# Rebuilding float32 weights from float64 words on Trainium2: the clamp of the high word left out, its scale changed, and a new order of work

## The chip, the cores and the metric

The kernel runs on one core of one Trainium2 chip. The metric is the device time of one execution in microseconds (us), the median of three runs: 724.92 us before the change (723.97 to 729.51). TensorE does the matrix products and transposes, VectorE (DVE in the profile) and ScalarE (ACT) the elementwise work, GpSimd (POOL) elementwise work that they can spare, and the queues of SyncE (SP) and ScalarE start the DMA transfers.

## The reference

A clustered attention feeds two dense blocks in a row. Queries and keys are assigned to the nearest of 16 centroids, and a query sees only the keys of its own cluster:

```python
q_assign = np.argmax(np.einsum('bhsd,hcd->bhsc', q_n, c_n), axis=-1)
k_assign = np.argmax(np.einsum('bhsd,hcd->bhsc', k_n, c_n), axis=-1)
mask = q_assign[:, :, :, None] == k_assign[:, :, None, :]
scores = np.where(mask, scale * np.matmul(q, k.transpose(0, 1, 3, 2)), -1000000000.0)
attn = softmax(scores)             # q, k, v: (2, 8, 768, 64)
x = attn @ v                       # as (1536, 512)
h = x @ w_in                       # (512, 2048)
g = np.where(h >= 1, h, np.where(h <= -1, 0.0, (h + 1) ** 2 / 4))
x = g @ w_out                      # (2048, 512)
h = ((x @ w1) * (x @ w2)) @ w3     # (512, 1024) twice, (1024, 1024)
return h @ w_out2                  # (1024, 512)
```

The activations are float32. The five weight matrices arrive as float64.

## The kernel before, in words

**Stages.** The work is cut by the two elements of the batch. Batch 0's attention comes first (four units of two heads; a unit has 12 score blocks of 128 queries by 768 keys). Beside it the kernel multiplies w3 by w_out2 once (the 16 products of line 1207). Then batch 0's dense work (line 1277: `h`, `y`, `ab` and `o` products) runs on TensorE with batch 1's attention mixed in, and last batch 1's dense work, in part as seven products for eight (line 1530). A score block goes TensorE (line 860), row maximum on VectorE (line 868), a bias on GpSimd (line 873), exponential on ScalarE (line 881), transposes on TensorE (line 898), a copy out of PSUM (line 353 on ScalarE, 355 on VectorE), and its PSUM buffer is then free for another. In batch 0 there are four such score buffers.

**A weight chunk.** A chunk is a 128x512 block of float64, that is 128x1024 words of 32 bits in a ring `w64` of five buffers early and three later. There are 72 such chunks: 8 of w_out2, 16 of w3 and 48 of the rest, which are rebuilt once, kept in DRAM (`wd`) and read back as float32 for batch 1. `chunk` (line 1098) makes these steps of each:

1. `wl` (line 1106): a DMA, started from ScalarE's queue, brings the 512 KB.
2. `wabs` (line 1112): ScalarE takes the absolute value of the high words, read as float32, times 2^16, into a buffer of the ring `wf`. The upper 8 of the 11 exponent bits of a float64 stand where a float32 has its exponent, so that this scale adds 16 to them.
3. `clamp` (line 1116, step `("wc", i, 0)`): VectorE (68 chunks) or GpSimd (4 chunks) holds the result between two powers of two, in place.
4. `wr` (line 1122): ScalarE scales and rounds the low words.
5. `shift_low` (line 1126): VectorE shifts the high word left by 3 bits and ORs the low word's bits in.
6. `sign` (line 1132): VectorE ORs the sign bit in. The 32 bits are then the weight as float32, and the `w64` buffer is free.
7. For a chunk that is multiplied at once: `whi` (lines 353 and 355) rounds it to TensorE's reduced float32 into a buffer of the ring `whl` (three buffers), on ScalarE or VectorE, and `wlo` (line 358) subtracts that from the weight, on GpSimd or VectorE.

**What sets the order.** Every step is handed to a small planner with the engines that may do it. `Plan.order` (line 127) then takes no decision of its own: it reads the string `ORDER` (lines 38 to 97), two letters a step, that says which step is next and on which of its engines. Engines run their instructions in that order, each on its own, and wait for each other by semaphores.

Of the kernel before, what the change touches and what calls it, by code (L numbers as in the profile page):

```python
# [38 lines left out]
    "###%#*#,#0#($V%X%[:m$X$.#.#2#6$0#4$6%e%h$8$:%V%b$<$_%c%q$a$>$c$e$4$2#g;#;4#_%]%_%i%y&,%|%k&#:s;D:o%m#L$H$@#m"  # L39
    "#8$J$g$B$L$Z$]$q$s$F;%;)$N;T&($D;*#B;:#o#X$*$i#q$o$P$u$k:q$m#|#@#P#e#w#k$R$%%s%u$T%w;J:u$w;6;F%o#y#c)u#a#J#<"  # L40
    "#N#F#D$()w)y$y$|)|:w:y:|*4;g;Z;,;.;y*(***,#>*##T*%*6*8;1;2$##]#i#R#V;8&**.*@*B*D*:%#;m*F#:*<;<*0;H;>;A;B*2*>"
    ";L#s*L*H*N*P*X#Z*Z*];V;X;i;N;k&&;o;Q;q*J$,#H#u*u;s*R*T+4&>*_*e;|<#*g;R*a*V*c+(+**w+6;];_*m<%<(<*<2&.+,*y&0&:"
    "*|+@+.+#+&+8+:+<<D<4<6;a;c<V+0+2+>+L&3*i*k<i+B+D+N+P+X+Z+]*o<8<:&7&5<<<>+F+R&G*q+_<F<H<-+e<.*s<y;e;v&K+H+T+u"
    "+a+J+V+c,(+w,4,6,*<J&8&<&I<]<X<k+m+y+|,#,L,8,:,,,.=2=%<Z<_<L<m&M<N<Q<R;w%>%(<a<c,0,%,2,@,B,D,X&N,N&D<o<q=D,<"
    ",>,Z<s<0<A<|=V,F<B=#=(,u,P,R+g+i+l=*,T,H+o=8,],_,a<u<w=i=4,J,V,w,y,|+r=J=6,e=:=<=,=.=>&Q<T<f<g-#-%,c&@-(-*+s"
    "-4-6=y=o>2=F=H-,-.&C-8,g=L=X=Z&c-:&j=0=@=B=N=]=_=a=c-0-2=P=R=k-@,i-<-L-B-D-X-Z-]>%&T>D-N-P=|>#=m&_-F->>(=q=s"
    ">V&k>4,k=u=w>8>i>*>,>.>6-R&X,m,o-H-u-K-w,r-y>:&S><>>=T=e=g>|-T,s%%.(.*%@-_>J>F-V>H>X>Z>L>]-|>_&W>a>c>N>0-a&e"
    "-c?4>@>k&o>B.#-e&^.4.6>m&a&[%*>Q.%>o>q>S>s&n?D.,..?(-m&s-g-i-k?:>u>w.8.0.@.B.D.3-o>T>f>g.L.N?T?#?%?*?6?8&g?,"
    "?.?<?F?H-q.:&u?g.F.X.<.P.R.T?J?Z?>?|?V.H.Z.J?L.W?X@4.>?N.]._>y?@?0.u?2.a?m.c%B?]?Q/4/(?_?a?C?S/@/6-s.w/B/*@H"
    "&y(&?u?c?e?w?y&q@Z(#@(?i&w(-%,@#?k@%&|?o(((.%D/8.y.|@6@8@*.e/:?q?s/,/./D@,@:@<.m@J@L@>@@/#/%@N@P@R/</0/2@o/>"  # L50
    "%.%0%2%4@.@0/F@T@V/L%F%H.g/N/P%6%J/H@BA(A<@a@]@`/J@u@i@2AN@D%L(*%8/R@q@F/X/Z(4.i.k/]%:.o@c@s%<%N@e@g/_/e@w/g"
    "/T/V@X@k.q.s@m/a/cABA*@y@|AcAuA./u0(/w/y0*/|0,0.A>A,A0A#APA604%P06%RA@A2A4%T/mARADAFATAVAXAZ08000#0%020:A%A8"
    "A:0<0@AHAK0>0L0N0PAe/i/k0XAiAg0B0DB0AkAmAp0u0wAqA|0R0FA]B*ALA_Aa0Z0]AwAyBBB#0T0HBV0J/o/rB20_0y0|B6AsB,B4B.(0"
    "1#0a0V1(0c(2/s0eB8B%B:(61*1,0gB(BDBF1416BHBi18BJBL0m1.10BXBZB]B_Ba1%BNBPB<B>121X1ZBw1]0i0kBd1:1@1L(:Be1N1P1B"
    "1DBk(8(=(>B@BRBT1RBo(A1<1T(B(L1FC#0o0r0s1_1>(NBm1e1gBqBg1H1J1VByB|1a1d(D(FCBBsBu(H(J1i1lC%2*2,2.201u1w1y1|(P"
    "(RCaD%23241m1o1r(T1s(V2#2%2628(XCDCG2(C(C*C,C.(ZCd2:2<C0C6C8C:C32>DD2F2HD)2JC52@2B2DD*C<C?C@GDCTCV2L2O2P2RCX"
    "CeCHCJCZDFCL2T2VDcCN2XD,D.D0D2CQE(2c2eE6C]2Z2]2gCR2i2_D4C_2lCsCuCwCyDH2a2mCgCiDeDh2oD8D:D6D<D>C|CkE*CmG_3%3("
    "3*DJDLDOD#3436E,3,3/3032DiDVE9EDGJER3P3R2y(]CoEaDPDkDADCCrE.383:3<3>3@DmDXD[D]Do3T3VE:F%D_3Y3Z3]3B3D3F(b(d(_"
# [35 lines left out]
    "hBgYjDiRhqiUh4hDg_gagZhuhwh,hyi_iai%h0h>h8isi(hHhLi4hFi[i^h:j)hsi,icieiwhki*jFjNhNiui6hPh~j,ihiii|hJhRilipjH"
    "imjahThVi8i:i.i>jPjdi<j.iBiDjeiFiqj*iyj#jLj0i0i@iHjRj%j6jJjgjij4j2j>j8j;j<jTjAjkjmjojBiJiLjZjqk#j^k.k&k@k)k*"
    "jwk,k0kBk3kEkHkFkJjyj|j_jWjXkLk:k<k>jtjukNk4kPkRk6k8kTkVkXkZ"
# [44 lines left out]
def cluster_attention_moe_kernel(  # L141
# [961 lines left out]

# [692 lines left out]
```

## Time and profile before

| | |
|---|---|
| median of the runs | 724.92 us (723.97 to 729.51) |
| profiled execution | 726.57 us, its span 724.9 us |
| busy share of the span | TensorE 97%, VectorE 87%, ScalarE 67%, GpSimd 39% |
| granted TensorE clock, mean | 0.998 of full speed |

The span runs from the first to the last instruction of the program; 1.7 us of the profiled execution lie around it. A TensorE that is shown busy is not one at its peak, since its instructions overlap and their ends are modelled. The shares are means over stages that differ: ScalarE is shown busy for 156.7 us of the 175 us from 25 to 200 us, and for 4.1 us of the last 25 us.

### The profile page before, as it was taken

The page shows a single profiled execution, that of the slowest core. Times are in us where ns is not written, and L with a number is a line of the kernel's source. Part 1 is how long each engine was busy: PE and PEld are TensorE (multiplying, and loading weights), DVE is VectorE, ACT ScalarE, POOL GpSimd, SP SyncE. Part 2 cuts the span into 40 slices and gives each one's busy share as a digit, 9 for nine tenths or more (in the row PEclk, how much of TensorE's full clock was granted, in tenths as well). Part 3 has the DMA queues.
Part 4 walks back from the last instruction along what each step waited for, and adds up shares of the span by engine and source line. Part 5 has one row for each costly group of instructions (what it writes and reads, how often), then busy time and mean ns, then how long its engine had stood idle before and what let it go on. Part 6 is the DMA issues. An engine that isn't in the chain of part 4 may idle for free.

```text
span 724.9 us, 12096 instructions
## 1 busy us (share of the span) xinstructions
PE 700.6 (97%) x4184; PEld 632.5 (87%) x4185; DVE 631.0 (87%) x1135; ACT 482.9 (67%) x897; POOL 283.4 (39%) x351
## 2 busy tenths in 40 slices
PE   4999999899999999999999999999999999999998
PEld 1867777577799999899989999999999999999997
DVE  6999999999988989999999999578988888999940
ACT  7989999988877897887877766335744444444201
POOL 3424334313544523522351532134644433267600
PEclk9999999999999999999999999999999999999999
DMA  8346687877789999897898788554212121222112
GB/s 315 97 158 218 215 260 234 278 236 235 198 200 204 198 218 222 205 246 196 217 225 248 212 207 216 140 171 147 74 58 74 59 87 45 60 70 62 58 44 102
DMA packets 122509, 121.58 MB, mean 168 GB/s; under 512 B 80656, under 2 KB 89296, under 8 KB 122448
## 3 DMA queue, kind: packets, MB, share of 16 engines
q1 hardware_dynamic: 99888, 61.39, 33.6%
q10 hardware_dynamic: 22560, 59.42, 26.4%
q8 instruction: 33, 0.54, 0.3%
q14 instruction: 28, 0.23, 0.1%
HBM read 75.79 MB, written 22.28 MB: 135 GB/s over the span
## 4 chain that ended last, share of the span: by engine, by line
PE 74%; DVE 6%; ACT 3%; issue 2%; DMA 0%; POOL 0%; DVEq 0%; SPq 0%; ACTq 0%; POOLq 0%
PE mo L1277 36%; PE sc L1277 7%; PE sc L1530 6%; PE sc L860 6%; PE mo L1530 5%; PE mo L1207 3%; PE av L977 3%; PE sc L898 2%; PE av L1277 2%; PE av L969 2%; PE av L1530 2%; ACT pt L353 1%; DVE wf L1132 1%; DVE tv L1441 1%; ACT P L881 1%
## 5 line engine op out<-in xcount | busy, mean ns | idle before, releaser
L1277 PE MATMUL mo<-X,whl 128*128 128x384 f32 x912 | 168.2, 339 | 0.6 <-DVE tmp L1302 0.4
L1277 PEld LDWEIGHTS mo<-X,whl 128*128 128x128 f32 x912 | 158.6, 188 | 3.7 <-DVE tmp L1302 0.7
L358 POOL TENSOR_TENSOR whl<-wf,whl 128x512 fp32r<-128x512 f32 x64 | 86.1, 1346 | 113.5 <-ACT whl L353 79.6
L1277 PE MATMUL mo<-G,whl 128*128 128x384 f32 x660 | 122.5, 340 | 0.2 <-DVE G L358 0.2
L1277 PEld LDWEIGHTS mo<-G,whl 128*128 128x128 f32 x660 | 116.0, 188 | 1.9 <-issue 0.6
L868 DVE TENSOR_REDUCE nm<-sc 128x1 f32<-128x768 f32 x96 | 89.6, 951 | 7.5 <-PE sc L860 6.5
L353 ACT ACTIVATE whl<-wf 128x512 fp32r<-128x512 f32 x84 | 52.5, 628 | 46.6 <-PE mo L1277 19.6
L873 POOL TENSOR_SCALAR nm<-nm 128x1 f32<-128x1 f32 x96 | 29.7, 310 | 132.2 <-DVE nm L868 128.2
L860 PE MATMUL sc<-k,q 128*128 128x512 f32 (+1 forms) x192 | 53.4, 359 | 5.4 <-ACT pt L353 2.7
L1122 ACT ACTIVATE w<-w,down 128x512 uint32<-128x512 uint32 x72 | 54.8, 768 | 0.4 <-ACT whl L353 0.3
L1112 ACT ACTIVATE wf<-w 128x512 f32<-128x512 f32 x72 | 47.9, 672 | 6.8 <-POOL whl L358 2.6
L1132 DVE SCALAR_TENSOR_TENSOR wf<-w,wf 128x512 uint32<-128x512 uint32 x72 | 51.6, 721 | 0.8
L1126 DVE SCALAR_TENSOR_TENSOR wf<-wf,w 128x512 uint32<-128x512 uint32 x72 | 50.0, 698 | 2.2 <-ACT w L1122 1.0
L881 ACT ACTIVATE P<-sc,nm 128x768 f32<-128x768 f32 x52 | 46.5, 900 | 7.3 <-POOL nm L873 1.9
L881 ACT ACTIVATE sc<-sc,nm 128x768 f32<-128x768 f32 x44 | 38.1, 867 | 19.4 <-POOL nm L873 19.2
L860 PE MATMUL sc<-kq 80*128 80x512 f32 (+1 forms) x192 | 49.5, 339 | 0.0
L358 DVE TENSOR_TENSOR phl<-sc,phl 128x768 f16<-128x768 f32 x44 | 41.9, 953 | 4.9 <-ACT phl L353 4.6
L898 PEld LDWEIGHTS sc<-ident,P 128*128 128x128 f32 x312 | 36.0, 143 | 11.1 <-ACT P L881 7.3
L898 PE MATMUL sc<-ident,P 128*128 128x128 f32 x312 | 42.6, 281 | 3.0 <-ACT P L881 2.7
L358 POOL TENSOR_TENSOR wh<-ws,wh 128x256 fp32r<-128x256 f32 x42 | 34.0, 817 | 25.5 <-ACT wh L353 14.8
L1277 PE MATMUL sc<-G,whl 128*128 128x384 f32 x240 | 43.7, 339 | 0.0
L1277 PEld LDWEIGHTS sc<-G,whl 128*128 128x128 f32 x240 | 42.5, 188 | 0.0
(241 smaller groups left out, 1478.0 us busy)
## 6 DMA issues: line engine op xcount, KB each, us to landing
wf<-wd ACTq DMA_DIRECT2D x64, 256.0 KB, 2.8
w<-in_w_out_dram ACTq DMA_DIRECT2D x24, 512.0 KB, 4.3
wd<-wf SPq DMA_DIRECT2D x48, 256.0 KB, 3.3
w<-in_w3T_dram ACTq DMA_DIRECT2D x16, 512.0 KB, 4.3
w<-in_w_in_dram ACTq DMA_DIRECT2D x16, 512.0 KB, 4.9
w<-in_w_dram ACTq DMA_DIRECT2D x16, 512.0 KB, 4.1
wp<-wf SPq DMA_DIRECT2D x16, 256.0 KB, 3.0
wf<-wp ACTq DMA_DIRECT2D x16, 256.0 KB, 2.9
```

The source lines that it names most:

```text
L353: nc.scalar.activation(out=out, in_=in_, func=AF.Copy)
L358: (nc.gpsimd if e == "POOL" else nc.vector).tensor_tensor(out=out, in0=a, in1=b, op=ALU.subtract)
L860: nc.tensor.matmul(ps[:, n], q[0:n_rows, q0:q0 + 128], k[0:n_rows, n], start=first, stop=not first)
L868: nc.vector.tensor_reduce(out=nm, in_=T[("sc", b), s], axis=AX.X, op=ALU.max, negate=True)
L881: nc.scalar.activation(out=new(("P", b), s).rearrange("p n s -> p (n s)") if by_pe(s) else T[("sc", b), s], in_=T[("sc", b), s], func=AF.E ...
L898: nc.tensor.transpose(T[("sc", b), s][:, c], p[:, c], ident)
L1112: nc.scalar.activation(out=T["wf", i], in_=T[w64, i].bitcast(F32)[:, :, 1], func=AF.Abs, scale=1.0 if by_add else float(2.0 ** 16))
L1122: nc.scalar.activation(out=lo, in_=lo, func=AF.Identity, scale=float(2.0 ** -29 - 2.0 ** -41), bias=down)
L1126: nc.vector.scalar_tensor_tensor(out=w, in0=w, scalar=3, in1=T[w64, i][:, :, 0], op0=ALU.logical_shift_left, op1=ALU.bitwise_or)
L1132: nc.vector.scalar_tensor_tensor(out=w, in0=T[w64, i][:, :, 1], scalar=0x80000000, in1=w, op0=ALU.bitwise_and, op1=ALU.bitwise_or)
L1277: nc.tensor.matmul(acc, w[:, a, k4 * 128:(k4 + 1) * 128], rhs(c, k4), start=(first and k4 == 0 and n == 0), stop=(last and k4 == 3 and n = ...
L1530: nc.tensor.matmul(ps, lhs(av, a, k), rhs(bv, c, k), start=k == 0 and n == 0, stop=k == 1 and n == 2,)
```

## The change

`wabs` scales by 2^-112 in place of 2^16. The eight exponent bits of the high word are thus brought down so far that a weight of ordinary size leaves the upper three of them zero, which the shift by 3 bits pushes out. The clamp is no longer made: `shift_low` now needs `wabs` itself and `wr`. The unused variant with `by_add` is deleted. The string `ORDER` is a new one, with 72 steps fewer, so that steps stand elsewhere on all engines, and some are done by another engine than before.

```diff
 ORDER = (
-    "###%#*#,#0#($V%X%[:m$X$.#.#2#6$0#4$6%e%h$8$:%V%b$<$_%c%q$a$>$c$e$4$2#g;#;4#_%]%_%i%y&,%|%k&#:s;D:o%m#L$H$@#m"
+    "###%#*#,#0#.$.$V%X#(%V%[#2$0#4%e%h%c%q$6$8$:$<$>$X$_$a$c$e%b%k$2$4$H%]:m:|%y&,%_%i;0;>$@$B$D%m;L$]$Z$q#B$g$i"
...
         def absv(e):
             new("wf", i)
-            nc.scalar.activation(out=T["wf", i], in_=T[w64, i].bitcast(F32)[:, :, 1], func=AF.Abs, scale=1.0 if by_add else float(2.0 ** 16))
-
-        def clamp(e):
-            w, x = T["wf", i], 1.0 if by_add else 2.0 ** 16
-            (nc.gpsimd if e == "POOL" else nc.vector).tensor_scalar(
-                out=w, in0=w, scalar1=float(x * 2.0 ** -15), scalar2=float(x * 2.0 ** 16 * 1.875), op0=ALU.max, op1=ALU.min
-            )
+            nc.scalar.activation(out=T["wf", i], in_=T[w64, i].bitcast(F32)[:, :, 1], func=AF.Abs, scale=float(2.0 ** -112))
...
             add(("wabs", i), {"ACT": 0.56}, t - 9.0, absv, [("wl", i)], [("wf", i)], behind="wf")
-            add(("wc", i, 0), {"DVE": 0.34, "POOL": (1.92, LATE)}, t - 8.6, clamp, [("wabs", i)])
...
-                add(("wc", i, 2), {"DVE": 0.6}, t - 7.8, shift_low, [("wc", i, 0), ("wr", i)])
...
+            add(("wc", i, 2), {"DVE": 0.6}, t - 7.8, shift_low, [("wabs", i), ("wr", i)])
```

The lines of the changed kernel are numbered lower: by 1 up to `chunk`, so that 355 becomes 354, by 5 at `wl` (1101) and by 11 at `shift_low` (1115) and `sign` (1121).

Two places show what the new `ORDER` does. The first is VectorE in batch 0's attention, from the product of the attention's output with its normalizer (`av<-av,rb`) to the low half of that output (`X_75<-av,X_75`), first before and then now:

```order
L988 TENSOR_TENSOR av<-av,rb 128x384
L1126 SCALAR_TENSOR_TENSOR wf<-wf,w_115 128x512
L355 CAST kq_105<-kq_119 64x768 x2
L1132 SCALAR_TENSOR_TENSOR wf<-w_115,wf 128x512
L355 CAST kq_106<-kq_119 64x768
L1116 TENSOR_SCALAR wf<-wf 128x512
L355 CAST whl<-wf 128x512
L937 TENSOR_SCALAR su<-su 128x6
L938 RECIPROCAL rc<-su 128x6
L358 TENSOR_TENSOR X_75<-av,X_75 128x384
```

And in the changed kernel, on the same engine between the same two steps (its lines 987 and 357):

```order
L987 TENSOR_TENSOR av<-av,rb 128x384
L867 TENSOR_REDUCE nm<-sc_178 128x1
L1115 SCALAR_TENSOR_TENSOR wf<-wf,w_115 128x512
L354 CAST whl<-wf 128x512
L354 CAST X_75<-av 128x384
L357 TENSOR_TENSOR whl<-wf,whl 128x512
L1121 SCALAR_TENSOR_TENSOR wf<-w_115,wf 128x512
L354 CAST kq_105<-kq_119 64x768
L357 TENSOR_TENSOR X_75<-av,X_75 128x384
```

The clamp (L1116) is gone, and in its place VectorE does the low half of a weight (`whl<-wf,whl`) beside its high half (`whl<-wf`), and the high half of the attention's output (`X_75<-av`).

The second place is ScalarE and its DMA queue at the very start, where `kq_105` to `kq_107`, `k_99` to `k_101` and `q_102` are rounded queries and keys, `w_113` to `w_115` the buffers of the ring `w64`, and `kq_119` the queries and keys as loaded. Before:

```order
L426 ACTIVATE rt<-ss 128x1
L353 ACTIVATE kq_105<-kq_119 64x768
L1106 DMA w_113<-in_w_out_dram 128x1024
L429 ACT_TABLE_LOAD
L429 ACTIVATE P_108<-ss 128x1
L353 ACTIVATE kq_106<-kq_119 64x768
L353 ACTIVATE k_99<-kq_119 64x768
L353 ACTIVATE k_100<-kq_119 64x768
L1106 DMA w_114<-in_w_out_dram 128x1024
L1106 DMA w_115<-in_w_out_dram 128x1024
```

In the changed kernel, on the same engine from the same step (line 425):

```order
L425 ACTIVATE rt<-ss 128x1
L428 ACT_TABLE_LOAD
L428 ACTIVATE P_108<-ss 128x1
L352 ACTIVATE kq_105<-kq_119 64x768
L352 ACTIVATE k_99<-kq_119 64x768
L352 ACTIVATE kq_106<-kq_119 64x768
L352 ACTIVATE k_100<-kq_119 64x768
L352 ACTIVATE kq_106<-kq_119 64x768
L352 ACTIVATE kq_105<-kq_119 64x768
L1101 DMA w_113<-in_w_out_dram 128x1024
L1101 DMA w_114<-in_w_out_dram 128x1024
```

The first weight load has moved from behind one rounding to behind six, and the exponential's table is loaded ahead of all of them.

## Rows read from the trace of the kernel before

**Rows 1.** The page's part 1: busy time and share of each engine.

```profile
PE 700.6 (97%) x4184; PEld 632.5 (87%) x4185; DVE 631.0 (87%) x1135; ACT 482.9 (67%) x897; POOL 283.4 (39%) x351
```

**Rows 2.** Windows: stretch, length, busy PE, PEld, DVE, ACT, POOL, then clock, DMA.

```profile
0.00:25.00 25.00, 15.25 (x100) 9.43 (x101) 17.56 (x42) 20.69 (x29) 9.32 (x17) 1.00 0.69 252
25.00:200.00 175.00, 166.06 (x992) 122.39 (x993) 165.85 (x272) 156.68 (x269) 63.21 (x87) 0.99 0.68 218
200.00:300.00 100.00, 100.00 (x612) 95.56 (x611) 89.61 (x144) 77.91 (x145) 44.16 (x56) 1.00 0.93 206
300.00:350.00 50.00, 48.64 (x314) 44.48 (x313) 48.94 (x83) 40.89 (x75) 14.68 (x20) 1.00 0.87 218
...
700.00:725.00 25.00, 21.45 (x122) 21.13 (x120) 3.90 (x7) 4.13 (x8) 1.29 (x1) 1.00 0.21 74
```

**Rows 3.** Waits of PE, 25 to 200 us: total us, times, longest.

```profile
PE sc L898 <- ACT P L881: 2.7, 4, 1.0
PE sc L860 <- ACT pt L353: 2.7, 7, 0.6
```

**Rows 4.** The chain that ended last, in time: start, us, what.

```profile
140.79 2.80 PE mo L1207 x12
...
166.82 1.31 PE sc L898 x12
...
174.77 4.02 PE av L969 x24
...
179.59 0.71 PE sc L860 x4
```

**Rows 5.** Groups by line, PE, 25 to 200 us: count, busy, mean ns, idle before.

```profile
L898 PE MATMUL sc<-ident,P 128*128 128x128 f32 x294 | 40.2, 281 | 3.0 <-ACT P L881 2.7
...
L969 PE MATMUL av<-pt,vn 128*64 128x384 f32 x192 | 32.7, 490 | 0.1
L860 PE MATMUL sc<-k,q 128*128 128x512 f32 (+1 forms) x100 | 29.1, 372 | 4.6 <-ACT pt L353 2.7 <-ACT P L881 1.6 <-DVE nm L868 0.2
...
L470 PE MATMUL av<-ident 128*128 128x128 f32 x28 | 4.1, 275 | 0.0
...
L581 PE MATMUL sc<-phl,tri 128*128 128x384 bf16 x1 | 0.3, 323 | 0.0
```

**Rows 6.** Windows of the clamp's line 1116 alone: stretch, DVE busy, POOL busy.

```profile
25.00:200.00 175.00, 16.16 (x37) 1.92 (x1) 0.99 0.68 218
200.00:450.00 250.00, 13.37 (x30) 3.88 (x2) 1.00 0.89 214
```

**Rows 7.** Groups by line, 25 to 200 us, DVE and then ACT.

```profile
L355 DVE CAST kq<-kq 64x768 fp32r<-64x768 f32 x7 | 3.8, 549 | 0.1
L355 DVE CAST whl<-wf 128x512 fp32r<-128x512 f32 x5 | 2.1, 422 | 0.1
L358 DVE TENSOR_TENSOR whl<-wf,whl 128x512 fp32r<-128x512 f32 x2 | 1.4, 686 | 0.0
...
L353 ACT ACTIVATE whl<-wf 128x512 fp32r<-128x512 f32 x13 | 8.2, 632 | 0.3 <-DVE wf L1132 0.2
L353 ACT ACTIVATE kq<-kq 64x768 fp32r<-64x768 f32 x7 | 5.9, 840 | 0.1
```

**Rows 8.** Groups by line, PE, 0 to 25 us.

```profile
L540 PE MATMUL sc<-kq,cT 128*32 128x384 f32 x32 | 6.2, 641 | 3.8 <-DMA kq<-in_kT_dram 2.2 <-DMA kq<-in_qT_dram 0.9 <-DVE P L556 0.7
```

**Rows 9.** The chain that ended last, from 293 us.

```profile
296.78 2.33 DVE wf L1132
```

**Rows 10.** Waits of the whole span: total us, times, longest.

```profile
ACT whl L353 <- PE mo L1277: 19.6, 8, 7.5
...
ACT whl L353 <- PE sc L1277: 17.3, 5, 5.8
```

**Rows 11.** Single lines: ns min/median/max of POOL's low halves and DVE's casts.

```profile
L358 POOL TENSOR_TENSOR whl<-wf,whl x64: 1273/1292/1892, 47.9 to 710.2; 128x512 fp32r<-128x512 f32 x64
...
L355 DVE CAST whl<-wf x16: 410/420/585, 56.4 to 444.1; 128x512 fp32r<-128x512 f32 x16
```

More of the change, by code (lines that the diff above doesn't have):

```diff
@@ L44 @@
[L44 to L58, printed above, removed]
@@ L94 @@
[L94 to L96 removed]
+    "###%#*#,#0#.$.$V%X#(%V%[#2$0#4%e%h%c%q$6$8$:$<$>$X$_$a$c$e%b%k$2$4$H%]:m:|%y&,%_%i;0;>$@$B$D%m;L$]$Z$q#B$g$i"
+    "#:#g$,$J$s$L$o$N:o%s$F%u%|;##L#o#y#<#a%w$m:q#N$##R;2$P$R#u&#&($k%o$T$u$w)u)w#@#F#H#8#V#i)y#X#J$y$|:s:u;B;%;("
@@ new lines @@
+    ":x:y*(*4***,)|*##k#_#D#>#T*6*8;P;4*%;];@;**.*@*B#q#Z#c#6#]#m$%#w*:*0*<%#*D*F*H;N;-;/;6*2*>;8;m;;;a<#;<*L*N*J"
+    "#|*X*Z*P*R$*#e$(#P#s*u;_;D;F;c;R;T;e;g*]*_<4+(*T*a*V*c*w*y+4&1;H;J+6+8+*+,<D;q&7;o;s*e*g&:;u*|<(+:<T*m+.;V;X"
+    "<H<%+@+#+B+&&2+D+0+<+2*i+L+N*k&**o+P+X+Z+]&%<X<*;x+F*r;z;Z+R+T+H<,<.&5+>*s+_+e+a+u&G&/&<%(+J+V<c+c+w+y;i;k&N"
+    ",4,(,*,,,6<6<F<J&9<L<N<8<:<<&E&I<?+m+|,#,.&K,8,:,<<s,%<V,0,2,><g&>%%<@,@,L=*=:<e,B,D+g,N,P,F,R,X,Z,],_<i<k<Z"
+    "<n<]<p,e,g<`<a;|<0<2,H,T,a,J<u+i+l,u,w=J<w=X<y<|+o=#%@&@&B<B<Q<R,V,c,y,|=,=<=i=>-(&P=.-#-*+r-,-.-4-6-%-8-:=0"
@@ L97 @@
+    "cwd.cyd0eXdkdieHeLeKe]eNeBeFd2f,f2egfyd,d8d5dwePeRdad6dyeZekd:d<fNdmfPe#d|eTe(f:f|f4f6f<f>f]f9fAg$g%eWdoe_f_"
+    "eifBfFfHe*gofJeaeme%eoe,e.e0eceseweeeufDfVe2eqf#fRfag(g*g,g.gsgqheg0gDgRg4g8fTf%guh:eze|g<g6g@gBfcf(fXfigxh%"
+    "g:h(gyh*gHgFh<fLg?gNfehhgVhIfmfgfZfofqg2gLgJhog|fkh-h.h0hBh$hjgXgThJh2h7fsh5i(h9g_hri2gcgfi*fuggfwiDh>hLhNgZ"
+    "g]hmhkh@i,hshDgPhThXiNgagii5h[h]hFi.i0hPhuhRi6i8hVh_hahxhyhcgkiagmh|i#iGiHikiPi:i<i%i>iJiSiLicimi@iBieigiiio"
+    "iqitiuiZi]i_iTiViXiwiyi|"
 )
@@ L1175, in chunk @@
             add(("wabs", i), {"ACT": 0.56}, t - 9.0, absv, [("wl", i)], [("wf", i)], behind="wf")
-            add(("wc", i, 0), {"DVE": 0.34, "POOL": (1.92, LATE)}, t - 8.6, clamp, [("wabs", i)])
-            if by_add:
-                add(("wc", i, 1), {"DVE": 0.34}, t - 8.2, rebase, [("wc", i, 0)])
-                add(("wc", i, 2), {"DVE": 0.6}, t - 7.8, top, [("wc", i, 1)])
-                add(("wr", i), {"ACT": 0.56}, t - 8.5, low_round, [("wl", i)])
-                add(("wc", i, 3), {"POOL": 1.37}, t - 7.0, low_add, [("wc", i, 2), ("wr", i)], frees=[(w64, i)])
-            else:
-                add(("wr", i), {"ACT": 0.56}, t - 8.5, low_floor, [("wl", i), "c_const"])
-                add(("wc", i, 2), {"DVE": 0.6}, t - 7.8, shift_low, [("wc", i, 0), ("wr", i)])
-                add(("wc", i, 3), {"DVE": 0.6}, t - 7.0, sign, [("wc", i, 2)], frees=[(w64, i)])
+            add(("wr", i), {"ACT": 0.56}, t - 8.5, low_floor, [("wl", i), "c_const"])
+            add(("wc", i, 2), {"DVE": 0.6}, t - 7.8, shift_low, [("wabs", i), ("wr", i)])
+            add(("wc", i, 3), {"DVE": 0.6}, t - 7.0, sign, [("wc", i, 2)], frees=[(w64, i)])
             last = ("wc", i, 3)
```

103 lines of the change are left out of this document (45 added, 58 removed).

## The prediction

> **What bounds the kernel now.** I began with the busy shares of the page. The reader sees TensorE busy for 700.6 of 724.9 us and VectorE for 631.0 [rows 1]. By this the change looks worth little: it takes work from an engine that has 94 us of idle time, and TensorE shows only 24 us that could be won. But these are means, so the next view is the windows by stage [rows 2]. From 200 to 300 us TensorE is busy for all of the 100 us and VectorE for 89.6: TensorE is the bound there, and work taken from VectorE wins nothing. From 25 to 200 us, batch 0's attention, it is the other way round: VectorE is busy for 165.85 of 175 us (94.8%), ScalarE for 156.68 (89.5%), and TensorE for 166.06. From 300 to 350 us VectorE is at 48.94 of 50 us and TensorE, at 48.64, loses 1.36. In the first 25 us it loses 9.75, in the last 25 us 3.55.
>
> The third view is what TensorE waits for in batch 0's attention: exponentials and copies of scores on ScalarE [rows 3]. ScalarE itself is fed by VectorE's row maxima and shares the copies with it, so these two are one resource here, and it is nearly full.
>
> How much TensorE could win there is not its idle 8.94 us, because its busy time counts overlapped and stretched instructions. The chain shows what its work takes when it runs packed: 2.80 us for the 12 products of a w3 step, 1.31 us for 12 transposes, 4.02 us for the 24 products of an attention output, 0.71 us for the four of a score block [rows 4]. In the stage stand the 16 w3 steps of line 1207 (44.8 us), 8 outputs (192 products, 32.2), 50 score blocks (100 products of the first kind, two a block, 35.5) and 294 transposes (32.1), and seven smaller groups, from 4.1 down to 0.3 us, that I take as they are shown, 16.4 us [rows 5]. That is 161.0 us of work in 175: the stage can shrink by 14 us at most before TensorE alone holds it.
>
> **The change part by part.**
>
> *The clamps.* Of the 68 on VectorE 37 lie in the stage, 16.16 us, or 0.437 us each, and 30 from 200 to 450 us, 13.37 us [rows 6]. The four on GpSimd go too; it is busy for 63 of 175 us in the stage [rows 2], so I count them at nothing; their cover is that idle time. ScalarE's absolute value stays one instruction with another constant, at no cost. The clamp stood between it and the shift, so a chunk is also ready earlier; nothing in rows 3 waits for chunks, and I count nothing for it.
>
> *The new order.* I counted what the two orders put ahead of the first product of line 1277, that is, what batch 0's attention and the w3 products need. VectorE loses 38 clamps (16.6 us). It takes over nine weight casts from ScalarE (0.422 us each, 3.8), three low halves from GpSimd (0.686, 2.1), a net four casts of queries and keys (0.549, 2.2) and one copy of a normalizer (0.55), and gives back two copies of 128x512 (1.4) [rows 7]. The balance is -9.4 us. ScalarE gives up the nine casts (0.632 each, 5.7), the four (0.840, 3.4) and the copy (0.55), and takes the two copies (1.3) and one of 128x768 (0.84): -7.5 us [rows 7]. TensorE has the same work to within one score block.
>
> If VectorE stays as full as it was, the stage takes (165.85 - 9.4) / 0.948 = 165.0 us, 10.0 less. If ScalarE is the measure, (156.68 - 7.5) / 0.895 = 166.7 us, 8.3 less. Both must be served, and I take -9. From the other side the bounds are TensorE's -14 and nothing. At -9 TensorE would be at 161 of 166, 97%, so little is left above this. The granted clock of 0.99 over the stage [rows 2] can give back 1% of it at most, 1.75 us; that is in the bounds, not in the sum.
>
> *A wait that the order adds.* A cast on VectorE waits for a buffer of the ring `whl`, which TensorE frees, and behind it stand the row maxima. The five casts in the stage cost 0.1 us of idle time in all [rows 7]. ScalarE's casts met long waits elsewhere: 8 and 5 of them, 19.6 and 17.3 us [rows 10]. I take 0 for the nine casts, with 36.9 / 13 = 2.8 us for one as the other end.
>
> *A rule weighed.* GpSimd's low halves took 1292 ns in the median and at most 1892, VectorE's weight casts 420 and at most 585 [rows 11]. The Trainium skill (SBUF — State Buffer, section "SBUF: two separate sides") says that VectorE and GpSimd share a pair of ports under an exclusive lock, so that whichever starts first blocks the other fully. By that rule a moved cast could stand for a whole low half. Nine casts and three subtractions of 1.29 us more would add 15.5 us and turn the gain into a loss. The rows agree that some instructions are stretched, but not by that: no cast was over 0.17 us longer than the median, which makes 2 us for the twelve. I leave the sum as it is.
>
> *The start.* TensorE's first products lost 2.2 and 0.9 us to loads of keys and queries [rows 8]. In the new order the first weight load stands behind six roundings instead of one, so the transfers of keys and queries share the DMA engines with less. It can win from 0 to 3.1 us; since VectorE's chain of masks runs beside them, I take -0.5.
>
> *Batch 0's dense work.* From 300 to 350 us TensorE loses 1.36 us [rows 2], and the chain of waits leaves TensorE there for VectorE, at the sign step of a chunk [rows 9]. Thirty clamps less, against some of the further casts that VectorE takes, should close most of that: -1, with -1.4 and 0 as bounds. What comes late next is TensorE itself.
>
> *Batch 1's dense work and the end.* No clamps are there. The order is another one, without a cause in either direction: 0, with 2 us either way.
>
> **Sum:** -9 - 0.5 - 1 = -10.5. The profiled execution took 726.57 us, so its like would take 716.1. It was 1.65 us above the median of 724.92, and the forecast for a median is 714.4 us.
>
> **Rivals.**
>
> 1. *The time stays.* What holds the attention may be the round trip of a score block through three engines and four buffers, not VectorE's load. For it: rows 3 name ScalarE alone, and VectorE never. Then only the part of those 5.4 us that ScalarE's relief of 5% touches is won, 0.3 us, and with no gain later the median is 724.6. Against it: ScalarE is relieved as well, and 94.8% of a stage is hardly a latency.
>
> 2. *All of it is won.* The attention runs at TensorE's pace (-14), the loads no longer hold the start (-3.1) and the middle closes (-1.4): 724.9 - 18.5 = 706.4. Against it: TensorE would have to be at 100% through three coupled engines, which the stage never showed.
>
> 3. *Slower.* VectorE takes more casts than the nine: 49 in place of 28 in the whole program. A cast that must wait for a `whl` buffer holds up every row maximum behind it, and TensorE, which frees the buffer, waits for those in turn. If the 21 waited for 0.5 us each on the path, the gain would be spent (10.5 us): 724.9; from there on it is a loss. If seven of them met what ScalarE's casts met, 2.8 us [rows 10], the time would be 724.9 - 10.5 + 19.6 = 734. Against it: the idle 0.1 us before the five [rows 7].
>
> **How the numbers follow.** The forecast has 0.66, rival 1 has 0.19, rival 2 has 0.07, rival 3 has 0.08. About 1% (7.2 us) can be told from no change by a measurement here, so faster by over 1% means under 717.7. Of the forecast's 0.66, 0.06 lie above that (its own range is 709 to 720). Faster: 0.60 + 0.07 = 0.67. Within 1%: 0.06 + 0.19 + 0.03 of rival 3 = 0.28. Slower by over 1%: 0.05. The range goes from rival 2 to within 2 us of rival 1: 706 to 723.
>
> **What would show each step right or wrong.** In the profile after, the first product of line 1277 should start some 9 us earlier than now, and VectorE's busy time up to then should be about 9 us less, with its share still near 95%. If that share falls well below and the start moves by under 3 us, rival 1 holds. If idle time stands before VectorE's `whl` casts, released by TensorE, rival 3 does. TensorE's loss from 300 to 350 us should be under 0.5 us, and the wait for keys before line 540 shorter. The prediction is wrong if the attention shrinks as said and the time is lost again after it: then a dense stage is not at TensorE's pace in the new order.

## The result and the profile after

The changed kernel took 719.46 us in the median of six runs (718.89 to 721.02), the kernel before beside it 726.88 us (723.97 to 731.36, six runs): a ratio of 0.991, with a 95% interval from 0.9881 to 0.9939. That is 0.9% less time, 0.6 to 1.2%. The forecast was 714.4 us: the direction is right, the time lies in the range of 706 to 723, and the gain is 7.4 us where 10.5 were forecast. Taken once more with the experiments (e4 below) the gain is 0.7%, 0.5 to 0.95%. The two profiled executions, 726.57 and 719.4 us, differ by 7.2 us. One run of a later kernel (e10, 731.93 us) was in a slower state of the chip and is left out. The ratios are those on record with their intervals; they can differ from the quotient of two medians by some 0.2%.

The page's part 1 of the changed kernel, to be held against [rows 1]:

```profile
PE 697.5 (97%) x4185; PEld 633.1 (88%) x4185; DVE 615.3 (86%) x1087; ACT 467.4 (65%) x873; POOL 279.6 (39%) x351
```

VectorE has 15.7 us less to do, ScalarE 15.5, and TensorE 3.1. The stages show where the time went. First the changed kernel in windows, with the columns of [rows 2]; the lines that end at 193.00 take the attention up to the first product of batch 0's dense work.

```profile
0.00:25.00 25.00, 14.45 (x82) 8.88 (x83) 17.00 (x39) 18.71 (x26) 7.12 (x15) 0.93 0.70 252
25.00:200.00 175.00, 170.26 (x1039) 128.06 (x1039) 163.26 (x257) 154.41 (x267) 61.15 (x87) 1.00 0.72 223
200.00:300.00 100.00, 98.53 (x597) 92.86 (x596) 90.82 (x148) 73.08 (x137) 34.22 (x47) 1.00 0.89 208
300.00:350.00 50.00, 50.00 (x326) 46.68 (x325) 46.62 (x76) 41.06 (x74) 24.01 (x28) 1.00 0.96 236
...
0.00:193.00 193.00, 177.72 (x1079) 130.11 (x1080) 173.98 (x286) 168.39 (x284) 66.74 (x99) 0.99 0.71 229
25.00:193.00 168.00, 163.26 (x999) 121.23 (x999) 156.98 (x248) 149.68 (x259) 59.62 (x84) 1.00 0.71 225
```

The same two stretches of the kernel before, where that product starts at 198.6 us:

```profile
0.00:198.60 198.60, 179.91 (x1082) 130.42 (x1084) 182.04 (x311) 176.54 (x296) 72.54 (x104) 0.99 0.69 223
25.00:198.60 173.60, 164.66 (x984) 120.99 (x985) 164.48 (x270) 155.85 (x268) 63.21 (x87) 0.99 0.68 219
```

Up to the first dense product VectorE is busy for 8.1 us less (182.04 to 173.98) and ScalarE for 8.15 less (176.54 to 168.39). The dense product itself, by its line in the changed kernel (1239) and, in the second fence, in the one before (1277):

```profile
L1239 PE MATMUL mo<-X,whl x912: 332/337/444, 193.0 to 713.9; 128*128 128x384 f32 x183
```

```profile
L1277 PE MATMUL mo<-X,whl x912: 333/337/446, 198.6 to 721.1; 128*128 128x384 f32 x183
```

It starts 5.6 us earlier, and the spans differ by 7.2 (724.9 and 717.7). So in these two executions the attention gives 5.6 us, and all that comes after it 1.6. One execution of each is not much: in the second profile of the changed kernel (e4) the product starts at 194.5 us, and each of the two executions here lost up to 1.7 us ahead of this product to a spell of TensorE's lower clock, the kernel before from 115 to 119 us, the changed one from 18 to 22 (see the last section).

What TensorE waits for from 25 to 193 us in the changed kernel, to be held against [rows 3]:

```profile
PE sc L897 <- ACT P L880: 2.3, 4, 1.1
PE sc L859 <- ACT pt L352: 1.2, 5, 0.3
PE mo L954 <- POOL tmp L944: 0.6, 1, 0.6
```

The engine waits for the same two things as before, exponentials and copies on ScalarE, 3.5 us where there were 5.4. With a third row of the kernel before, also for exponentials, which [rows 3] doesn't show, there were 7.0:

```profile
PE sc L860 <- ACT P L881: 1.6, 2, 1.3
```

### The profile page after: what moved, and what is told of

It reads as the page before. It is cut to its first block, busy times and chain, and to the rows that moved or that the text cites. A ratio compares the mean times of both kernels' runs of the same rounds, so it can differ in the third digit from the quotient of the medians.

```text
span 717.7 us, 12011 instructions
## 1 busy us (share of the span) xinstructions
PE 697.5 (97%) x4185; PEld 633.1 (88%) x4185; DVE 615.3 (86%) x1087; ACT 467.4 (65%) x873; POOL 279.6 (39%) x351
## 4 chain that ended last, share of the span: by engine, by line
PE 80%; ACT 5%; DVE 5%; issue 2%; DMA 1%; ACTq 0%; POOL 0%; SPq 0%; DVEq 0%; POOLq 0%
PE mo L1239 37%; PE sc L1492 9%; PE sc L859 7%; PE mo L1492 6%; PE sc L1239 5%; PE av L976 3%; PE mo L1169 3%; PE av L1239 3%; PE sc L897 2%; PE av L968 2%; PE av L1492 2%; ACT P L880 2%; DVE nm L867 1%; ACT pt L352 1%; DMA wf<-wp 1%
## 5 line engine op out<-in xcount | busy, mean ns | idle before, releaser
L357 POOL TENSOR_TENSOR whl<-wf,whl 128x512 fp32r<-128x512 f32 x69 | 92.0, 1335 | 128.4 <-DVE whl L354 53.6
L1239 PE MATMUL mo<-G,whl 128*128 128x384 f32 x684 | 126.2, 339 | 0.0
L1239 PEld LDWEIGHTS mo<-G,whl 128*128 128x128 f32 x684 | 120.4, 188 | 0.8 <-ACT phl L352 0.3
L352 ACT ACTIVATE whl<-wf 128x512 fp32r<-128x512 f32 x63 | 39.3, 628 | 36.8 <-PE mo L1239 19.0
L897 PE MATMUL sc<-ident,P 128*128 128x128 f32 x312 | 40.7, 275 | 2.4 <-ACT P L880 2.3
L352 ACT ACTIVATE pt<-sc 128x768 f32<-128x768 f32 (+1 forms) x46 | 36.4, 811 | 5.8 <-PE sc L897 4.7
L859 PEld LDWEIGHTS sc<-k,q 128*128 128x128 f32 x192 | 31.5, 189 | 9.0 <-ACT pt L352 3.7
L357 DVE TENSOR_TENSOR whl<-wf,whl 128x512 fp32r<-128x512 f32 x43 | 31.0, 721 | 9.2 <-ACT whl L352 8.7
```

What stands on the lines that cost most here:

```text
L352: nc.scalar.activation(out=out, in_=in_, func=AF.Copy)
L357: (nc.gpsimd if e == "POOL" else nc.vector).tensor_tensor(out=out, in0=a, in1=b, op=ALU.subtract)
L859: nc.tensor.matmul(ps[:, n], q[0:n_rows, q0:q0 + 128], k[0:n_rows, n], start=first, stop=not first)
L897: nc.tensor.transpose(T[("sc", b), s][:, c], p[:, c], ident)
L1239: nc.tensor.matmul(acc, w[:, a, k4 * 128:(k4 + 1) * 128], rhs(c, k4), start=(first and k4 == 0 and n == 0), stop=(last and k4 == 3 and n = ...
```

## The experiments

The prediction's theory was that the load of VectorE and ScalarE sets the attention's length. Against it stand three others: that the sequence sets it, since each engine does its instructions in a fixed order and waits in it for the others; that the move of casts from ScalarE to VectorE is what the new order wins by; and that TensorE's packed work does. The expectations give the times by each: the loads are theory 1 or L (S, where ScalarE's alone is meant, and the moved casts with it), the sequence is theory 2 or O, TensorE's work T. Each kernel is compared with runs of the kernel before on the same chip.

**The two halves apart.** There are two edits, the clamp left out and the new order, and so four kernels: these two, and the two that have one edit alone. The first keeps the order of before without its 72 clamp steps:

```diff
 ORDER = (
-    "###%#*#,#0#.$.$V%X#(%V%[#2$0#4%e%h%c%q$6$8$:$<$>$X$_$a$c$e%b%k$2$4$H%]:m:|%y&,%_%i;0;>$@$B$D%m;L$]$Z$q#B$g$i"
+    "###%#*#,#0#($V%X%[:m$X$.#.#2#6$0#4$6%e%h$8$:%V%b$<$_%c%q$a$>$c$e$4$2#g:|;0#_%]%_%i%y&,%|%k&#:q;>:o%m#L$H$@#m"
...
```

> The old order with its 72 clamp steps struck out and nothing else moved; the scale is the new one. If VectorE's load itself held batch 0's attention (theory 1), the 16.6 us of clamps there are worth 4 to 9 us with ScalarE unrelieved: 718 to 723 us, and the first product of line 1277's kind (dense work of batch 0) starts 4 to 9 us before 198.6 us. If the gain is the new order's, because each score block's round trip holds the stage (theory 2), the time stays within 2 us of before, about 725 to 727 us, and VectorE only idles more.

The second has the new order, with the scale of 2^16 (`by_add` is False) and the clamp on VectorE, a step directly ahead of each shift:

```diff
-            nc.scalar.activation(out=T["wf", i], in_=T[w64, i].bitcast(F32)[:, :, 1], func=AF.Abs, scale=float(2.0 ** -112))
+            nc.scalar.activation(out=T["wf", i], in_=T[w64, i].bitcast(F32)[:, :, 1], func=AF.Abs, scale=1.0 if by_add else float(2.0 ** 16))
...
+            add(("wc", i, 0), {"DVE": 0.34, "POOL": (1.92, LATE)}, t - 8.6, clamp, [("wabs", i)])
```

> The new order with a clamp put back on VectorE ahead of each shift (72 of them, old scale). Theory 1: VectorE has 17 us more to do in batch 0's attention, where it is 93% busy, and the gain of 7 us is lost or turned round: 726 to 734 us. Theory 2 (the order carries the gain, a clamp hides in VectorE's waits): 720 to 723 us.

The third is the changed kernel with its first 180 steps, up to the seventh score block at about 35 us, in the order of before; the fourth is the changed kernel once more, for its time on this chip.

```diff
 ORDER = (
-    "###%#*#,#0#.$.$V%X#(%V%[#2$0#4%e%h%c%q$6$8$:$<$>$X$_$a$c$e%b%k$2$4$H%]:m:|%y&,%_%i;0;>$@$B$D%m;L$]$Z$q#B$g$i"
+    "###%#*#,#0#($V%X%[:m$X$.#.#2#6$0#4$6%e%h$8$:%V%b$<$_%c%q$a$>$c$e$4$2#g:|;0#_%]%_%i%y&,%|%k&#:q;>:o%m#L$H$@#m"
...
```

> The changed kernel with its first 180 steps (all engines, up to the seventh score block, some 35 us) in the old order, less the clamps, and the rest in the new one. Theory: the new start lost about 2 us of TensorE's work by 25 us (packed work begun by then 9.1 us against 11.1) and the half clock that now falls there; undone, the time is 1.5 to 3 us under the changed kernel's, 716.5 to 718. Rival: the start is taken up by later waits and the time stays at 719 to 720.

> The changed kernel once more beside the others, unaltered: 719 to 720 us by every theory, the measure for the other three on the same chip.

The kernel before took 725.04 us here (23 runs).

| order | clamp | us | ratio, 95% interval |
|---|---|---|---|
| old | made | 725.04 (722.37 to 732.16) | 1 |
| old | left out (e1) | 724.21 (721.5 to 727.85) | 0.9993 (0.9973 to 1.0012) |
| new | made (e2) | 742.04 (740.9 to 743.78) | 1.0244 (1.022 to 1.0268) |
| new | left out (e4) | 719.69 (718.78 to 725.5) | 0.9929 (0.9905 to 0.9953) |
| new, first 180 steps old | left out (e3) | 718.02 (717.38 to 719.28) | 0.991 (0.9892 to 0.9929) |

Neither edit alone wins anything that can be told from noise. The clamps left out are worth nothing measurable in the old order (the interval leaves room for 2 us), and 22 us in the new one (742.04 - 719.69), with the clamps where this kernel has them; other places for them were not tried. The 742.04 us are beyond what either theory gave for e2. Windows of the kernel that leaves out the clamps alone, up to its first dense product at 196.3 us:

```profile
0.00:25.00 25.00, 17.13 (x104) 11.09 (x105) 18.21 (x43) 21.33 (x30) 7.41 (x16) 1.00 0.70 252
25.00:196.30 171.30, 162.02 (x979) 118.80 (x980) 150.66 (x231) 154.67 (x267) 62.67 (x86) 1.00 0.67 221
```

VectorE is busy for 150.66 of 171.3 us, 88%, where it was 94.7% before. (This profiled execution took 723.11 us, 1.1 under its median, and that of before 1.5 over. Its clock is 1.00 throughout, where that of before has the spell at 115 us: of the 2.3 us between 196.3 and 198.6 up to 1.7 are that, and the rest is within what the runs of one kernel differ by.) What the clamps took it now spends in waits (total us, times, longest; the same kernel, 25 to 196.3 us):

```profile
DVE nm L867 <- PE sc L859: 6.7, 9, 1.6
...
PE sc L897 <- ACT P L880: 3.3, 4, 1.1
...
DVE wf L1115 <- ACT w L1111: 2.5, 4, 1.3
```

Row maxima now wait for TensorE's scores and shifts for ScalarE's low words, while TensorE still waits for exponentials. In the kernel with the new order and the clamps VectorE is full, 172.45 of 180 us to the first dense product at 205.0:

```profile
25.00:205.00 180.00, 164.75 (x985) 119.19 (x986) 172.45 (x285) 150.30 (x257) 56.31 (x83) 1.00 0.64 210
```

So the load decides where the sequence leaves it no room; where it does, less load wins little or nothing.

**The moved casts.** In this stage eleven casts of weights that the old order does on ScalarE are done on VectorE in the new one (two go the other way, hence the nine of the prediction). The fifth kernel is the first one above (old order, no clamps) with these eleven on VectorE, where they stand in the sequence. Two of them, in the old order on VectorE:

```diff
 L987 TENSOR_TENSOR av<-av,rb 128x384
+L354 CAST wo_122<-wf 128x512
 L867 TENSOR_REDUCE nm<-sc_177 128x1
...
 L1121 SCALAR_TENSOR_TENSOR wf<-w_115,wf 128x512
+L354 CAST whl<-wf 128x512
```

> The old order without clamps, in which 11 of the weight casts of batch 0's attention go from ScalarE to VectorE, at the same places in the sequence, as the new order has them. Theory S (once the clamps are gone ScalarE holds the stage, and the gain comes from the work that VectorE takes off it): 11 times 0.63 us, 6.9 us of ScalarE's work, so 717 to 721 us. Rival O (a sequence fits the load that it was searched for, and the sequence itself is what gains): 723 to 726 us, as without the move.

The sixth is the changed kernel with them back on ScalarE. Two of them, on ScalarE:

```diff
 L880 ACTIVATE P_109,su<-sc_179,nm 128x768
+L352 ACTIVATE whl<-wf 128x512
+L352 ACTIVATE wo_122<-wf 128x512
 L352 ACTIVATE wf<-mo_128 128x512
```

> The changed kernel with the same 11 weight casts put back on ScalarE at their places. Theory S: ScalarE has 6.9 us more to do in the stage, 724 to 728 us. Rival O: VectorE is relieved by 4.6 us instead and the time stays at 719 to 721 us.

Beside 725.82 us of the kernel before, the fifth took 727.33 us (724.49 to 731.93), a ratio of 1.0021 (0.9997 to 1.0044), and the sixth 736.15 us (733.38 to 739.87), 1.0139 (1.0102 to 1.0175). The fifth is above what either theory gave for it. The casts win nothing in the old order, so their move by itself is not the gain; but the new order can't do without it. Back on ScalarE they cost some 16 us, for 6.9 us of work (11 of 632 ns, [rows 7]); that is more than any theory had said. The waits of the sixth kernel up to its first dense product (207.6 us):

```profile
DVE nm L867 <- PE sc L859: 11.7, 8, 6.2
...
ACT whl L352 <- DVE wf L1121: 7.6, 4, 4.1
...
PE sc L897 <- ACT pt L352: 5.4, 2, 4.8
```

A cast now holds ScalarE for up to 4.1 us until VectorE has put the sign in; a copy of scores stands behind it, TensorE waits up to 4.8 us for the copy, and VectorE's next maximum up to 6.2 for TensorE. The longest of all three are one event, between 105 and 115 us. The three waits close a circle, and one late step is paid more than once. A part is TensorE's clock: after it stood still from 107.6 to 112.3 us, the window from 110 to 118 has a mean of 0.57, which costs 3.4 us at most, and all six runs of this kernel have a mean clock of 0.998 or less.

```profile
110.00:118.00 8.00, 5.68 (x18) 4.83 (x19) 2.29 (x3) 7.97 (x15) 3.08 (x3) 0.57 0.70 211
```

**Loads taken away.** The next two kernels take work off one engine each, in the new order. The seventh leaves out the sign step of the 40 chunks that are built early, so their weights have no sign; the eighth leaves out the rounding of their low words, and ANDs them in raw. Each cut takes some 25 us from its engine up to the first dense product: VectorE's busy time falls from 173.98 to 149.66 us in e7, ScalarE's from 168.39 to 143.79 in e8.

```diff
         def sign(e):
+            if i < N_EARLY:
+                return
```

> The changed kernel without the sign step of the 40 early chunks (they keep the magnitude alone): 40 times 0.69 us, 27 us, less for VectorE in batch 0's attention, nothing moved. Theory S: within 2 us of the changed kernel, 717.5 to 720. If VectorE's load still holds the stage: 710 us or less, TensorE's packed work allowing some 9 us.

```diff
         def low_floor(e):
+            if i < N_EARLY:
+                return
...
-                out=w, in0=w, scalar=3, in1=T[w64, i][:, :, 0], op0=ALU.logical_shift_left, op1=ALU.bitwise_or
+                out=w, in0=w, scalar=3, in1=T[w64, i][:, :, 0], op0=ALU.logical_shift_left, op1=ALU.bitwise_and if i < N_EARLY else ALU.bitwise_or
```

> The changed kernel without ScalarE's rounding of the low words of the 40 early chunks; their shift then ANDs the raw low word in, at the same cost. 40 times 0.77 us, 30 us, less for ScalarE in batch 0's attention, nothing moved. Theory S: 709 to 714 us. If ScalarE's load does not hold the stage: 718 to 720 us.

The ninth has both cuts, and the tenth both cuts in the old order without clamps.

```diff
         def low_floor(e):
+            if i < N_EARLY:
+                return
...
         def sign(e):
+            if i < N_EARLY:
+                return
```

> The changed kernel without the sign step and without the rounding of the low words of the 40 early chunks: 27 us less for VectorE and 30 us less for ScalarE in batch 0's attention, nothing moved. If the loads of the two held the stage in turns (theory L), freeing both shows it: 712 us or less. If the fixed sequence and the round trip of a score block hold it (theory O): 715.5 to 718, as with the rounding alone left out.

> The old order without clamps, with the same two steps of the 40 early chunks left out. Theory L: 712 us or less, as in the new order, since the loads are the same. Theory O: the old sequence has a floor of its own above the new one's, 719 to 722 us, some 4 us above the new order with both steps out.

The seventh and eighth ran beside the fifth and sixth (725.82 us), the ninth and tenth beside 724.68 us of the kernel before.

| kernel | taken away | us | ratio, 95% interval |
|---|---|---|---|
| e7, new order | 25 us of VectorE | 719.86 (719.31 to 720.38) | 0.991 (0.9877 to 0.9943) |
| e8, new order | 25 us of ScalarE | 717.23 (716.31 to 719.83) | 0.988 (0.9845 to 0.9915) |
| e9, new order | both | 717.47 (716.72 to 718.2) | 0.9896 (0.9869 to 0.9924) |
| e10, old order | both | 721.57 (719.87 to 722.94) | 0.9939 (0.9902 to 0.9976) |

The eighth came out near what was said for a load that doesn't hold the stage, not at the 709 to 714 us of theory S. A window of the ninth, up to its first dense product at 191.0 us, and one of the tenth, up to 193.2:

```profile
25.00:191.00 166.00, 161.59 (x989) 120.26 (x989) 131.55 (x205) 125.81 (x220) 57.40 (x83) 1.00 0.70 229
```

```profile
25.00:193.20 168.20, 160.59 (x976) 118.31 (x976) 125.86 (x191) 132.06 (x231) 60.92 (x86) 1.00 0.69 226
```

In the ninth VectorE is down to 79% and ScalarE to 76%, and the stage is 2.0 us shorter than in the changed kernel. By load over share, as the prediction priced the clamps, 25 us off each of the two would have taken the attention down to TensorE's floor of 161. The two orders stay 4.1 us apart without these loads (721.57 and 717.47; 3.1 by the ratios), as they were 4.5 apart with them (724.21 and 719.69): most of what the new order wins on the old one does not come from the engines' loads. The intervals of the ninth and tenth just overlap, those of the first and fourth do not. In single profiles the stage from 25 us is 2.2 us longer in the tenth than in the ninth (168.2 and 166.0), and 3.3 longer in the first than in the changed kernel (171.3 and 168.0), so the rest of the difference lies elsewhere.

**A shorter round trip.** The eleventh kernel leaves GpSimd's bias out of the 48 score blocks of batch 0, which takes a step of some 0.3 us (in the changed kernel's profile 0.19 in the median and 0.37 in the mean of the 50 before 193 us) out of the way of each block; the exponentials then take the row maximum unscaled.

```diff
         def fn(e):
+            if s < NU:
+                return
             nc.gpsimd.tensor_scalar(out=tl[s, "nm"], in0=tl[s, "nm"], scalar1=SCALE, scalar2=EC, op0=ALU.mult, op1=ALU.add)
```

> The changed kernel without GpSimd's bias step in batch 0's attention (the exponential takes the negated maximum unscaled): the round trip of each of the 48 score blocks is 0.3 us shorter, with the loads of VectorE and ScalarE unchanged. If the round trip holds the stage: 715 to 718 us. If it does not: 719 to 720.5.

It took 721.5 us (719.35 to 724.31) beside the same 724.68 us, a ratio of 0.9959 (0.9942 to 0.9976): no gain on the changed kernel, and above what either theory said. A miss for the theory that the round trip of a score block is what counts by itself.

**TensorE's work.** The last kernel adds a third cut to the ninth: of the twelve products of each w3 step (three for each of four pairs of tiles) it makes four, so 128 products fewer, by [rows 4] 128 x 2.80 / 12 = 30 us of packed work.

```diff
-                for n, (a, c) in enumerate(PASSES):
+                for n, (a, c) in enumerate(PASSES[:1]):
...
-                        start=(k4 == 0 and n == 0), stop=(k4 == 3 and n == 2),
+                        start=(k4 == 0 and n == 0), stop=(k4 == 3 and n == 0),
```

> The changed kernel without the sign step and the low words' rounding of the 40 early chunks (as e9_new_both_off, 717.5 us) and with one of the three products of each weight step of w3 (line 1207 before): 128 matmuls, 30 us at the packed pace, less for TensorE in batch 0's attention. If TensorE holds the stage once the other two are free (theory T): 8 us or more under e9_new_both_off, 709 us or less. If the round trip of the score blocks through the fixed sequence holds it (theory O): within 3 us, 714.5 to 718.

It took 714.42 us (712.97 to 715.73) beside 725.59 us of the kernel before: a ratio of 0.9852 (0.9825 to 0.988), 3 us under the ninth's 717.47: just under the 714.5 that theory O allowed, and 5 above the 709 of theory T. Its window up to the first dense product, at 186.1 us, and then what its engines wait for in it:

```profile
25.00:186.10 161.10, 136.92 (x859) 95.98 (x858) 130.99 (x205) 124.96 (x220) 56.96 (x83) 0.99 0.72 236
```

```profile
PE sc L897 <- ACT P L880: 14.6, 13, 1.9
DVE nm L867 <- PE sc L859: 10.9, 15, 1.5
ACT pt L352 <- PE sc L897: 9.0, 12, 1.5
...
ACT P L880 <- DVE nm L867: 6.6, 5, 2.0
...
ACT P L880 <- POOL nm L872: 5.5, 6, 1.5
```

With 25, 25 and 30 us off three engines (30 as packed work; TensorE's busy time falls by 25) the stage is 6.9 us shorter than in the changed kernel (168.0 to 161.1), and no engine is above 85% of it. TensorE waits for exponentials, these for maxima and biases, the maxima for TensorE's scores: a circle in which no engine is the bound. The DMA is not it either: it stands behind 2.6 us of the waits of VectorE and ScalarE here, behind 1.8 in the ninth, and behind none of TensorE's. So TensorE's packed work holds some 5 us of what is left in the ninth kernel (166.0 to 161.1), and the sequence all below that.

## Why the prediction was right, and where its size was off

**What bounds the kernel.** Batch 0's attention was the place: 5.6 of the 7.2 us of the two profiles come from there (4.1 by the second profile of the changed kernel, e4). TensorE is busy there for 163.26 of 168 us, 97.2%; the prediction had put it at 97% for a stage of 166.

**The clamps and the new order.** The counts of work were right: VectorE lost 8.1 us before the first dense product against 9.4 forecast, ScalarE 8.15 against 7.5. What failed is the step that made time of them, "if VectorE stays as full as it was", and its like for ScalarE: load divided by a busy share, -9 us, where the profiles have -5.6 with the start in it. In the changed kernel the shares did stay near what they were, 93.4% and 89.1%, and the forecast of 95% for VectorE looked nearly met. Yet the shares are no cause: with the old sequence and the 38 clamps gone (13.2 us of busy time less up to the first dense product), VectorE fell to 88% and nothing measurable was won (e1); with 25 us less on each of the two in the new sequence, 2 us (e9). A busy share of 95% on an engine that also waits in a fixed order showed work that fits between the waits, not a bound. What was won came from the new sequence, for which the clamps had to go first: with them it costs 17 us. That the sum came within 5 us is luck in part: the term that makes 9 of its 10.5 us was worked out by a step that doesn't hold, and took for granted that the new order would use what the clamps leave free.

**Rival 1** was the better theory for the removal: it gave 724.6 us for a gain that isn't taken, and leaving the clamps out alone took 724.21. It was wrong in holding that no sequence could use what was freed; and its own mechanism, the length of one round trip, is not borne out by e11. **Rival 2** had the attention at TensorE's pace, -14. Neither order comes there: 50 us off the other two engines left the stage at 166.0 us (e9). **Rival 3** had VectorE's casts waiting for buffers of the ring `whl`. There are 49 of them now. The group of the changed kernel, whole span (count, busy, mean ns, idle before):

```profile
L354 DVE CAST whl<-wf 128x512 fp32r<-128x512 f32 x49 | 22.6, 461 | 0.4 <-PE mo L1239 0.3
```

Their idle time is 0.4 us in all. The value of 0 that the sum took for this wait was right.

**The rule that was weighed**, and put aside because no cast was over 0.17 us longer than the median [rows 11], was put aside on a wrong reading. A cast of VectorE does stand still until a subtraction of GpSimd that had begun before it ends; the longest cast of those rows began only 0.3 us ahead of such an end. The casts of the changed kernel (ns min/median/max), and the worst one with the subtraction that had begun just ahead of it (start, us):

```profile
L354 DVE CAST whl<-wf x49: 388/419/1458, 52.8 to 692.4; 128x512 fp32r<-128x512 f32 x49
```

```profile
291.19 1.30 POOL L357 TENSOR_TENSOR whl<-wf,whl 128x512 fp32r<-128x512 f32 x1 [4.17 <-ACT whl L352]
291.31 1.46 DVE L354 CAST whl<-wf 128x512 fp32r<-128x512 f32 x1
```

The subtraction ends at 292.48 us and the cast 0.28 us later. Three more of the 49 are held so (764, 700 and 834 ns); each ends 0.28 or 0.29 us after the end of the GpSimd instruction that ran when it began. The four cost 2.1 us together. None of them lies in batch 0's attention, where the longest cast took 448 ns, so the sum didn't suffer; in e5 one did, for 1397 ns.

**The start** went the other way: -0.5 was forecast. In the profiles, by 25 us TensorE has begun 82 products, where it was 100 [rows 2], and the first attention output, which needs the first score blocks, starts 0.6 us later. Single line 968 of the changed kernel, then 969 of the kernel before (first and last start):

```profile
L968 PE MATMUL av<-pt,vn x192: 486/486/537, 41.2 to 192.0; 128*64 128x384 f32 x192
```

```profile
L969 PE MATMUL av<-pt,vn x192: 485/486/537, 40.6 to 196.8; 128*64 128x384 f32 x192
```

The loads of keys no longer stand before the first products, as forecast, but other waits took their place. The group of [rows 8] in the changed kernel:

```profile
L539 PE MATMUL sc<-kq,cT 128*32 128x384 f32 x32 | 6.2, 759 | 4.9 <-DMA kq<-in_qT_dram 2.5 <-DVE cT L450 1.7 <-DVE P L555 0.7
```

It waits 4.9 us where it was 3.8: for queries, 2.5 us, and for VectorE's centroids, 1.7. With the old start the first output stands at 39.8 us and TensorE has begun 104 products by 25 us, at a clock of 1.00 (e3, its window and its line 968):

```profile
0.00:25.00 25.00, 17.03 (x104) 10.56 (x105) 18.11 (x43) 21.24 (x30) 7.41 (x16) 1.00 0.70 252
```

```profile
L968 PE MATMUL av<-pt,vn x192: 486/486/537, 39.8 to 191.4; 128*64 128x384 f32 x192
```

That kernel (e3) took 718.02 us against 719.69 of the changed one on the same chip, and is the fastest here that does all of the work, at the upper end of what its theory gave. It beats the kernel before; its interval and that of the changed kernel overlap, so the 1.7 us between them are not shown to be a gain.

**Batch 0's dense work** was forecast at -1, and -1.2 came: from the first dense product to the first of batch 1 the profiles have 301.1 us before and 299.9 after. From 300 to 350 us TensorE now loses nothing, for 1.36 [rows 2], but from 200 to 300 it loses 1.47 us that it didn't lose, 1.4 of them in two waits for VectorE. **Batch 1 and the end** gave -0.4, for 0.

**What stays open.** That the sequence holds most of the attention, and not the load of VectorE or ScalarE, follows from e1, e7 to e10 and e12: the loads were taken away and the time stayed within 3 us (some 5, with 30 us of TensorE's work gone as well). Which waits of it do is not settled; a shorter step in the round trip (e11) changed nothing for the better. TensorE's pace and the circle of waits lie within 5 us of each other, so one experiment on either shows little.

## What to carry to other kernels

Where engines work through fixed sequences and wait for each other, the price of a removed instruction can't be had from an engine's busy share: leave it out in the old sequence, and try the new sequence with it still in. Here neither edit alone won anything measurable, and both together won 0.7 to 0.9%, so the freed time had to be bought by a new order. Adding work to an engine that the sequence leaves no room can cost more than the work itself: 6.9 us of casts on ScalarE cost 16. And a profile is one execution: look for spells of the lower clock in both before a stage is said to have won or lost a microsecond or two.

## What the runs showed of the hardware

TensorE's granted clock fell for a while in the first 25 us of the changed kernel, which the kernel before doesn't show there [rows 2]. The profile of the kernel before has its own spell in the attention, after TensorE stood still from 111.95 to 113.24 us for an exponential:

```profile
112.00:113.00 1.00, 0.00 (x0) 0.00 (x0) 1.00 (x2) 1.00 (x3) 0.83 (x1) 1.00 0.72 82
115.00:119.00 4.00, 3.99 (x17) 3.72 (x18) 3.32 (x6) 3.05 (x5) 0.57 (x1) 0.57 0.74 236
```

The changed kernel in windows of 1 us (clock third from the end), then e7, which has the same order there less the sign steps:

```profile
15.00:16.00 1.00, 0.00 (x0) 0.00 (x0) 0.70 (x2) 0.96 (x2) 0.00 (x0) 1.00 1.04 412
16.00:17.00 1.00, 0.18 (x4) 0.19 (x8) 0.20 (x1) 0.97 (x2) 0.00 (x0) 1.00 1.05 416
17.00:18.00 1.00, 1.00 (x11) 0.38 (x4) 0.00 (x0) 0.95 (x3) 0.00 (x0) 1.00 1.00 399
18.00:19.00 1.00, 1.00 (x8) 1.00 (x6) 0.70 (x2) 1.00 (x2) 0.31 (x1) 0.63 0.77 306
19.00:20.00 1.00, 1.00 (x6) 1.00 (x6) 0.94 (x3) 0.18 (x1) 1.00 (x1) 0.50 0.20 78
20.00:21.00 1.00, 1.00 (x7) 1.00 (x6) 0.97 (x2) 0.26 (x1) 0.51 (x1) 0.50 0.00 0
21.00:22.00 1.00, 1.00 (x8) 1.00 (x8) 0.97 (x2) 1.00 (x2) 0.00 (x0) 0.66 0.00 0
```

```profile
15.00:16.00 1.00, 0.00 (x0) 0.00 (x0) 0.64 (x2) 0.97 (x2) 0.00 (x0) 1.00 1.03 404
16.00:17.00 1.00, 0.41 (x4) 0.23 (x8) 0.00 (x0) 0.95 (x3) 0.00 (x0) 1.00 1.05 417
17.00:18.00 1.00, 1.00 (x8) 0.00 (x0) 0.00 (x0) 0.98 (x2) 0.00 (x0) 1.00 1.02 409
18.00:19.00 1.00, 1.00 (x8) 0.91 (x5) 0.00 (x0) 0.76 (x2) 0.72 (x1) 1.00 0.66 262
```

In the changed kernel TensorE stands still for 2.5 us, from 14.3 to 16.8; it then works without a break, and from 18 us the clock falls to the lower level of 1.2 GHz (0.50, and 0.63 and 0.66 in the windows in which it falls and rises) until some time before 22. In e7 it stands still for 2.7 us, to 16.6, and the clock stays at 2.4 GHz. So the length of the pause alone doesn't tell which way it goes, and these runs leave open what does. Four microseconds at a mean of 0.57 lose 1.7 us of TensorE's full pace at most, in either profile. The times of the changed kernel don't show that loss: of its eighteen runs (e4's with them) the nine at a mean clock of 0.999 or more have a median of 719.44 us, the nine at less one of 719.53. So the 1.7 us by which e3 is faster, all of whose runs are at 0.999 or more, are not shown to be the clock's.
